# Value matmuls in rounds of four heads, a third bank that VectorE may take, projections issued singly, and 60 transposes by DMA

## The chip, the cores and the metric

The kernel runs on one core of a Trainium2 chip. Five engines work side by side and wait for each other through semaphores: TensorE (PE) for matmuls, ScalarE (ACT) for activations, VectorE (DVE), GpSimd (POOL) and SyncE (SP), which here only issues DMAs. PE writes to PSUM, eight banks of 512 fp32 values in each of 128 partitions. ACT and DVE read it. The metric is device time in microseconds of one execution.

## The reference, cut to what matters

Four layers on a sequence of 2048 tokens of width 512: attention (A), linear attention (B), A, B, each with a layernorm ahead and a residual behind.

```python
x = A_x                                    # [1, 2048, 512], bf16
x = x + _A_ref(_layernorm(x), A_wq, A_wk, A_wv, A_wo)
x = x + _B_ref(_layernorm(x), B_wqkv, B_wo)
x = x + _A_ref(_layernorm(x), A_wq, A_wk, A_wv, A_wo)
x = x + _B_ref(_layernorm(x), B_wqkv, B_wo)

# A: 32 query heads of 16, one shared key and value head
scores = einsum("bhqd,bkd->bhqk", q, k) * 16 ** -0.5
o = einsum("bhqk,bkd->bhqd", softmax(scores), v);   A = o @ wo
# B: phi(t) = where(t > 0, t + 1, exp(t)) + 1e-6
kv = einsum("bhsd,bhse->bhde", phi(k), v);  z = sum_s phi(k)
o = (phi(q) @ kv) / (phi(q) @ z + 1e-6);            B = o @ wo
```

An A layer needs 32 × 2048 × 2048 exponentials. They are most of the kernel's work.

## The kernel before, in words

An A layer is cut into *blocks*: 128 keys against 512 queries of one head, so one 128x512 tile of scores, one PSUM bank. A *segment* (`Seg`) is four heads (`j` = 0 to 3, one for each 32-row strip of TensorE) of one group `g` and one parity, for one stretch of 512 queries `qb`: 16 key tiles x 4 heads = 64 blocks. For `qb` = 0 the keys come in four passes, so that work starts before all keys are known, and those segments have 16 blocks. Each A layer has 2048 blocks, the two together 4096.

Each block goes through a score matmul (line 556, here QK), an exponential and a value matmul (line 568, here PV).

- Banks 0 to 5 form two *sets* of three. `act_stream` (line 581) takes a set, picks three blocks of three heads, issues their QK matmuls as one op, and one exponential on ACT over the three banks (line 627) into one of five `PT` buffers.
- With the QK op a fourth block may go to bank 7. DVE computes its exponential: one pass out of PSUM (line 683, `sV`) for each block, and three passes over pairs of blocks (lines 702, 704, 706) into a `DPT` buffer. `dve_open` (line 666) allows it only if bank 7 is free and nobody waits for it. These blocks come from the next two segments.
- Bank 6 (`ACC`) holds the sums of the value matmuls of the segment at hand, one 32-partition strip for each head. `pv` (line 559) makes one PE op of the blocks of one `PT` buffer (three heads) or of one `DPT` buffer (one or two), and hands it to the planner at once, before their exponentials are done. When all blocks of a segment are handed in, `norms` (line 716) queues the copy or addition out of bank 6 on DVE (lines 727, 729), and `norm` (line 735) *takes a general bank at that moment*, for four transposes (line 742), a reciprocal and a product (lines 750, 754).
- Bank 7 is the only general bank while sets are claimed. Everything else uses it in turn: layernorm transposes (`ln_tile`, line 465), projections (`mm`, line 455, four matmuls in one op), `norm`, the transposes of the attention output (`epilogue`, line 760), and the B layers (`run_b`, line 802).

The order on each engine is fixed when the program is built. A small simulator (`Planner`) runs the kernel with assumed durations (a QK op 0.52 us, a PV op 0.5 us) and, whenever an engine is free, gives it the ready op of the lowest priority number: 0 for QK, 0.5 for `norm`, 2 for PV and `sV`, 3 to 5 for most projections, 8 for DVE's long passes. A few copies (`copy_flex`, line 452) go to ACT or DVE, whichever is free first. On the chip each engine keeps that order, and waits where its inputs are late. B layers are fed as their tiles of x become ready, so most of a B layer runs beside the A layer before it. Only the last 512 rows do not.

Of the kernel before, what the change touches and what calls it, by code (L numbers as in the profile page):

```python
# [17 lines left out]
P = 128  # L18
# [9 lines left out]
class Op:  # L28
    __slots__ = ("eng", "opts", "fn", "deps", "prio", "left", "users", "done", "end", "n", "value", "sem", "signal", "isdma", "name")
# [8 lines left out]
class Planner:  # L38
# [3 lines left out]
    def __init__(self, nc):  # L42
        self.nc = nc
        self.now = 0.0
        self.events = []
        self.seq = 0
        self.ready = {e: [] for e in ENGS}
        self.busy = {e: False for e in ENGS}
        self.order = {e: [] for e in ENGS}
# [10 lines left out]
    def op(self, opts, reads=(), writes=(), prio=5.0, lat=0.08, dma=False, name=""):  # L60

        o = Op()
        o.opts, o.prio, o.users, o.done, o.end = opts, prio, [], False, None
        o.eng, o.fn, o.n, o.value, o.sem, o.signal, o.isdma = None, None, None, None, None, False, dma
        o.name = (name, lat)
        deps = set()
# [18 lines left out]
        o.left = 0  # L85
        for d in deps:
            if not d.done:
# [4 lines left out]
        return o  # L92

# [7 lines left out]
    def _dispatch(self, e):  # L101
        if self.busy[e]:
            return
        h = self.ready[e]
        while h:
            _, _, o = heapq.heappop(h)
            if o.eng is not None:
                continue
            dur, fn = o.opts[e]
            o.eng, o.fn = e, fn  # L110
            self.order[e].append(o)
            self.busy[e] = True
            self.at(self.now + dur, lambda: self._freed(e))
            self.at(self.now + dur + o.name[1], lambda: self._done(o))
            return

    def _freed(self, e):
        self.busy[e] = False
        self._dispatch(e)
# [89 lines left out]
    def finalize(self):  # L209
# [9 lines left out]
        for e in ENGS:  # L219
            c = 0  # L220
            for o in self.order[e]:
                if o.isdma:
                    o.sem = self.nc.alloc_semaphore("s_dma%d" % self.ndma)
                    self.ndma += 1
                    o.value = 16
                elif o.signal:
                    c += 1
                    o.sem, o.value = self.sems[e], c

    def emit(self, e, eng):  # L230
        waited = {}
        for o in self.order[e]:
            need = {}
            for d in o.deps:
                if not d.isdma and d.eng == e and e not in (DV, AC, PO):
                    continue
                k = ("dma", id(d)) if d.isdma else d.eng
# [12 lines left out]
class Seg:  # L250
    def __init__(self, i, qb, g, par, kts, first, last):
# [4 lines left out]
        self.submitted = 0  # L256
        self.emitted = [0] * 4
# [13 lines left out]
QK_DUR = 0.52  # L271
PV_DUR = 0.5
DMAX = 0.5
GA = 3
# [11 lines left out]
def bass_interleave_layers__grouped_kv_mqa__linear_attn_block__prompt_kernel(  # L286
# [32 lines left out]
    NXN = 4  # L319
# [31 lines left out]
    OB = sb("OB", [P, 2, D], BF16)  # L351
    OTB = sb("OTB", [P, 2, 4, P], BF16)
# [14 lines left out]
    banks = Pool_([7, 0, 1, 2, 3, 4, 5])  # L367
    sets = Pool_([])
    retire = {}
    got = {0: [], 3: []}  # L370
    plain_give = pl.give

    def give(pool, item):
        if pool is banks and retire.get(item):
            base = 0 if item < 3 else 3
            got[base].append(item)
            if len(got[base]) == 3:
                got[base] = []
                plain_give(sets, base)
# [5 lines left out]
    def claim_sets():  # L385
        for b in range(6):
            retire[b] = True
        held = [b for b in banks.free if b < 6]
        banks.free = [b for b in banks.free if b >= 6]
# [65 lines left out]
    def mm(dst, pairs, reads, b, prio, dur, stop=True):  # L455
        def fn(e):
            ins = None
            for k, (l, r) in enumerate(pairs):
                ins = e.matmul(dst, lhsT=l, rhs=r, start=(k == 0), stop=(k == len(pairs) - 1))  # L459
            return ins  # L460
        return op({PE: (dur, fn)}, reads=reads, writes=[B_(b)], prio=prio, lat=0.2)
# [3 lines left out]
    def ln_tile(t, prio):  # L465
# [9 lines left out]
           reads=[("x", t), ("mv", t), ("rs", t)], writes=[("xn", i)], prio=prio)  # L475
        b = yield ("acq", banks, prio)
# [13 lines left out]
    def a_tile(L, t, prio):  # L490
        yield ("flag", ("x", L - 1, t))
        yield from ln_tile(t, prio)
# [5 lines left out]
        pl.flag(("V", L, t))  # L498

# [41 lines left out]

    def run_a(L):
# [16 lines left out]
        def pv(sg, items, key, pool, it, holders):  # L559

            yield ("flag", ("acc", L, sg.i))
            for kt, _, _ in items:
                yield ("flag", ("V", L, kt))

            def fn(e):
                ins = None
                for kt, j, ap in items:
# [4 lines left out]
            o = op({PE: (PV_DUR, fn)}, reads=[key] + [("V", kt) for kt, _, _ in items], writes=[B_(ACC)], prio=2.0, lat=0.2)  # L572
            holders[0] -= 1
            holders[1].append(o)
            if holders[0] == 0:
                pl.give_after(pool, it, holders[1])
            sg.submitted += len(items)
            if sg.submitted == sg.total:
                pl.flag(("pv", L, sg.i))

        def act_stream():
            yield from need(segs[0])
            claim_sets()
            while True:
                s_ = yield ("acq", sets, 0.0)
                group = []
                while len(group) < GA and state["si"] < len(segs):
# [22 lines left out]
                extra = dve_open({g_[2] for g_ in group})  # L610
# [10 lines left out]
                op({PE: (QK_DUR, qkx)}, reads=reads, writes=wr, prio=0.0, lat=0.2)  # L621
                if extra is not None:
                    dve_take(extra)
# [5 lines left out]
                pl.give_after(sets, s_, [ex])  # L629
                parts = {}  # L630
                for i, (sg, kt, j) in enumerate(group):
                    parts.setdefault(sg.i, []).append((kt, j, PT[:, p_, i * 512:(i + 1) * 512]))
                hold = [len(parts), []]
                for si, items in parts.items():
                    pl.process(pv(segs[si], items, ("PT", p_), pt_pool, p_, hold))
# [3 lines left out]
        def finish():  # L639
            n = 0  # L640
            while n < 2:
                s_ = yield ("acq", sets, 0.0)
                for b in range(s_, s_ + 3):
# [22 lines left out]
        def dve_open(js):  # L666
            if not USE_DVE or not banks.free or banks.wait:
# [11 lines left out]
        def dve_take(extra):  # L679
# [5 lines left out]
                   writes=[B_(b), ("sV", c_, h)], prio=2.0, lat=0.25)  # L685
            pl.give_after(banks, b, [o])
            if h == 1:
                dve_close()

        def dve_close():  # L690
# [18 lines left out]
            parts = {}  # L709
            for h, (sg, kt, j) in enumerate(blk):  # L710
                parts.setdefault(sg.i, []).append((kt, j, DPT[:, d_, h * 512:(h + 1) * 512]))
            hold = [len(parts), []]
            for si, items in parts.items():
                pl.process(pv(segs[si], items, ("DPT", d_), dp_pool, d_, hold))

        def norms():
            for sg in segs:
                pl.flag(("acc", L, sg.i))
                yield ("flag", ("pv", L, sg.i))
# [15 lines left out]
        def norm(sg, src, key, a_):  # L735
# [3 lines left out]
            def tr(e):  # L739
                ins = None  # L740
                for c in range(4):
                    ins = e.transpose(ps[:, b * 512 + c * P:b * 512 + (c + 1) * P], src[:, c * P:(c + 1) * P], identF[:])  # L742
                return ins
            o = op({PE: (0.8, tr)}, reads=[key, "identF"], writes=[B_(b)], prio=pr, lat=0.2)
# [7 lines left out]
            dst = Osb[:, sg.qb % 2, :].rearrange("p (c g j r d) -> p g r j c d", c=4, g=4, j=4, r=2)[:, sg.g, sg.par]  # L752
# [7 lines left out]
        def epilogue(qb):  # L760
            crit = qb == NB - 1
            pr = 1.0 if crit else 4.0
            for g in range(4):
                for par in range(2):
                    yield ("flag", ("O", L, qb, g, par))
                b = yield ("acq", banks, pr)
                v = bank_bf(b)

                def tr(e, g=g, v=v):
                    ins = None  # L770
                    for c in range(4):
                        ins = e.transpose(v[:, c, :], Osb[:, qb % 2, c * D + g * P:c * D + (g + 1) * P], ident[:])  # L772
# [29 lines left out]
    def run_b(L):  # L802
# [13 lines left out]
        def tile_(t):  # L816
            pr = base(t // 4) + 0.01 * t
            yield ("flag", ("x", L - 1, t))
            yield from ln_tile(t, pr)
# [59 lines left out]
        def main(t):  # L879
# [5 lines left out]
            for h in range(2):  # L885
# [17 lines left out]
                pl.give_after(banks, b, [o])  # L903
            b = yield ("acq", banks, pr)
            v = bank_bf(b)

            def tr(e):
                ins = None
                for g in range(4):
# [5 lines left out]
            b = yield ("acq", banks, pr)  # L915
            m = mm(bank(b), [(OTB[:, i, g, :], wo2[:, g, :]) for g in range(4)], [("OTB", i), "wo2"], b, pr, 0.9)
            pl.give_after(ob_pool, i, [m])
            o = op({DV: (0.62, lambda e: e.tensor_tensor(out=x_sb[:, t, :], in0=x_sb[:, t, :], in1=bank(b), op=ALU.add))},
                   writes=[B_(b), ("x", t)], prio=pr)
            pl.give_after(banks, b, [o])  # L920
            pl.flag(("x", L, t))
# [9 lines left out]
    ob_pool = Pool_(range(2))  # L931
# [48 lines left out]
```

## Time and profile before

| | us |
|---|---|
| three runs: median (lowest to highest) | 2001.18 (1987.07 to 2008.94) |
| the profiled execution: its time | 1994.11 |
| the profiled execution: its span | 1992.4 |
| mean clock granted to TensorE, share of full | 0.734 |

A row of a group gives engine, operation, what is written from what, shapes, count, then the busy time in us, the mean of one in ns, and the idle time just before with what ended it. Busy time counts overlapping instructions once: ACT starts the next instruction before the last has ended, so busy time divided by the count is the pace, and the mean is the latency. A row of stretches gives its bounds and length, then busy us and number of instructions of each engine, the granted clock, and the DMA's share and rate. A row of the timeline gives start, length, engine, line, operation and count of merged instructions, with the idle time before it in brackets.

### The profile page before, as it was taken

Reading aid. Unit: us, or ns where it says so; the run is one execution under the profiler, and the core shown is the slowest. Engines: PE = TensorE matmul, PEld = TensorE weight load, DVE = VectorE, ACT = ScalarE, POOL = GpSimd, SP = SyncE. Lnnn points to the kernel's source line nnn. Section 1 sums busy time; section 2 is a strip of 40 time slices with the busy share of each in tenths; the row PEclk is TensorE's granted clock in tenths of the full one; section 3 lists DMA queues with packets and bytes.
Section 4 is the critical chain, followed back from the end, with each engine's and each line's share of the span. In section 5 each row is a group of like instructions: output and inputs, shape, how many; then the busy total and the mean of one; then the engine's idle time right before and its main releaser. Section 6 shows DMA issues by size and latency. Waiting matters only on the chain.

```text
span 1992.4 us, 25401 instructions
## 1 busy us (share of the span) xinstructions
PE 1631.2 (82%) x10138; PEld 449.5 (23%) x10208; DVE 1209.9 (61%) x1824; ACT 1783.4 (90%) x1392; POOL 40.2 (2%) x89
## 2 busy tenths in 40 slices
PE   7887887888788887887788888878887888878887
PEld 2211222112211122112322222221122111221123
DVE  5389235777387755776544452357763778457757
ACT  7899999999999989996489999999999999899952
POOL 2000000000000000000000000000000000000000
PEclk8857687657966687767778876976679556976668
DMA  3000000000000000000000000000000000000001
GB/s 107 1 1 1 1 1 1 1 1 1 1 1 1 1 1 1 1 1 0 1 1 1 1 1 0 1 1 1 1 1 1 1 1 1 1 1 1 1 1 43
DMA packets 7749, 9.00 MB, mean 5 GB/s; under 512 B 1488, under 2 KB 7120, under 8 KB 7632
## 3 DMA queue, kind: packets, MB, share of 16 engines
q1 hardware_dynamic: 7632, 7.37, 1.1%
q8 instruction: 81, 1.33, 0.3%
q14 instruction: 36, 0.29, 0.0%
HBM read 5.28 MB, written 2.10 MB: 4 GB/s over the span
## 4 chain that ended last, share of the span: by engine, by line
ACT 40%; PE 33%; issue 17%; DVE 9%; DMA 0%; POOL 0%; ACTq 0%; SPq 0%; POOLq 0%
ACT PT L627 37%; PE ps L568 10%; PE ps L556 10%; PE ps L459 7%; PE ps L742 3%; ACT phE L808 2%; DVE sQ L702 1%; DVE sQ L704 1%; DVE sV L683 1%; DVE accS L727 1%; PE ps L772 1%; DVE st L466 1%; DVE phR L809 1%; DVE DPT L706 1%; PE ps L893 1%
## 5 line engine op out<-in xcount | busy, mean ns | idle before, releaser
L627 ACT ACTIVATE PT<-ps 128x1536 bf16<-128x1536 f32 x1264 | 1726.1, 1527 | 87.8 <-PE ps L568 72.3
L556 PE MATMUL ps<-QT,KM 32*128 32x512 bf16 x4096 | 660.8, 501 | 257.8 <-ACT PT L627 236.9
L568 PE MATMUL ps<-PT,V 128*32 128x512 bf16 x3790 | 665.3, 494 | 5.3 <-DVE ve L468 3.1
L556 PEld LDWEIGHTS ps<-QT,KM 32*128 32x128 bf16 x4096 | 134.3, 96 | 806.7 <-ACT PT L627 611.3
L683 DVE TENSOR_SCALAR sV<-ps 128x512 f32<-128x512 f32 x306 | 210.5, 688 | 164.6 <-PE ps L556 164.3
L568 PEld LDWEIGHTS ps<-PT,V 128*32 128x32 bf16 x3790 | 130.9, 98 | 382.8 <-issue 361.7
L704 DVE SCALAR_TENSOR_TENSOR sQ<-sQ,sV 128x1024 f32<-128x1024 f32 (+1 forms) x164 | 189.1, 1153 | 5.5
L702 DVE SCALAR_TENSOR_TENSOR sQ<-sV 128x1024 f32<-128x1024 uint16 (+1 forms) x164 | 189.0, 1153 | 4.9
L706 DVE SCALAR_TENSOR_TENSOR DPT<-sQ,sV 128x1024 int16<-128x1024 f32 (+1 forms) x164 | 187.8, 1145 | 1.0
L809 DVE TENSOR_SCALAR phR<-ps 128x512 f32<-128x512 f32 x64 | 44.0, 691 | 146.8 <-ACT phE L808 146.8
L568 PE MATMUL ps<-DPT,V 128*32 128x512 bf16 x306 | 85.8, 559 | 2.5 <-DVE sacc L729 2.2
L459 PE MATMUL ps<-wqkv,xnT 128*128 128x512 bf16 x233 | 62.9, 395 | 18.4 <-DVE phR L809 12.8
L470 POOL TENSOR_TENSOR rs<-ve,mhalf 128x1 f32<-128x1 f32 x64 | 35.2, 551 | 1891.4 <-DVE ve L468 1882.6
L729 DVE TENSOR_TENSOR sacc<-sacc,ps 128x512 f32<-128x512 f32 x48 | 32.8, 684 | 56.9 <-PE ps L568 56.8
L727 DVE COPY accS<-ps 128x512 f32<-128x512 f32 x48 | 33.1, 690 | 50.3 <-PE ps L568 50.2
L750 DVE RECIPROCAL rden<-ps 128x16 f32<-128x16 f32 x64 | 16.5, 258 | 70.2 <-PE ps L742 69.2
L808 ACT ACTIVATE phE<-ps 128x512 f32<-128x512 f32 x64 | 44.0, 688 | 14.2 <-PE ps L459 13.8
L742 PE MATMUL ps<-identF,accS 128*128 128x128 f32 x192 | 48.0, 398 | 7.9 <-DVE accS L727 7.5
L453 ACT COPY OTB<-ps 128x512 bf16<-128x512 bf16 x20 | 11.7, 585 | 40.9 <-PE ps L910 40.9
L459 PE MATMUL ps<-wo,OTB 128*128 128x512 bf16 x110 | 38.6, 479 | 9.9 <-ACT OTB L453 6.8
L466 DVE BATCH_NORM_STATS2 st<-x_sb 128x6 f32<-128x512 bf16 x64 | 43.6, 684 | 2.9 <-DMA x_sb<-in_A_x_dram 1.9
L482 PE MATMUL ps<-ident,xn 128*128 128x128 bf16 x256 | 27.8, 241 | 20.5 <-DVE xn L473 11.9
(79 smaller groups left out, 759.9 us busy)
## 6 DMA issues: line engine op xcount, KB each, us to landing
out_dram<-x_sb SPq DMA_DIRECT2D x16, 128.0 KB, 1.7
x_sb<-in_A_x_dram SPq DMA_DIRECT2D x3, 512.0 KB, 6.1
wqkv<-in_B_wqkv_dram SPq DMA_DIRECT2D x1, 1536.0 KB, 11.3
x_sb<-in_A_x_dram SPq DMA_DIRECT2D x4, 128.0 KB, 2.3
wq<-in_A_wq_dram SPq DMA_DIRECT2D x1, 512.0 KB, 3.9
wo<-in_A_wo_dram SPq DMA_DIRECT2D x1, 512.0 KB, 8.0
wo<-in_B_wo_dram SPq DMA_DIRECT2D x1, 512.0 KB, 11.3
wk<-in_A_wk_dram SPq DMA_DIRECT2D x1, 16.0 KB, 2.2
```

The costliest lines, as they stand in the source:

```text
L459: ins = e.matmul(dst, lhsT=l, rhs=r, start=(k == 0), stop=(k == len(pairs) - 1))
L466: op({DV: (0.66, lambda e: e.bn_stats(st[:, t, :], x_sb[:, t, :]))}, reads=[("x", t)], writes=[("st", t)], prio=prio)
L556: return e.matmul(bank(b), lhsT=KM[r, sg.par, kt * P:(kt + 1) * P], rhs=QT[r, sg.g, sg.qb * 512:(sg.qb + 1) * 512], start=True, stop=True)
L568: ins = e.matmul(ps[32 * j:32 * j + 32, ACC * 512:(ACC + 1) * 512], lhsT=V[:, kt, :], rhs=ap, start=(sg.emitted[j] == 0), stop=(sg.emitted ...
L627: ex = op({AC: (0.05 + 0.4267 * n, lambda e, n=n, s_=s_, p_=p_: e.activation(PT[:, p_, 0:n * 512], ps[:, s_ * 512:(s_ + n) * 512], ACTF.Ex ...
L683: o = op({DV: (0.60, lambda e: e.tensor_scalar(out=sV[:, c_, h * 512:(h + 1) * 512], in0=bank(b), scalar1=VB, scalar2=VLO, op0=ALU.add, op ...
L702: op({DV: (t_, lambda e: e.scalar_tensor_tensor(out=qq, in0=fr, scalar=CA, in1=fr, op0=ALU.add, op1=ALU.mult))}, reads=keys, writes=[("sQ" ...
L704: op({DV: (t_, lambda e: e.scalar_tensor_tensor(out=qq, in0=qq, scalar=CB, in1=fr, op0=ALU.add, op1=ALU.mult))}, reads=keys, writes=[("sQ" ...
L706: o = op({DV: (t_, lambda e: e.scalar_tensor_tensor(out=DPT[:, d_, 0:n].bitcast(I16), in0=qq, scalar=CK, in1=vv, op0=ALU.mult, op1=ALU.add))},
L742: ins = e.transpose(ps[:, b * 512 + c * P:b * 512 + (c + 1) * P], src[:, c * P:(c + 1) * P], identF[:])
L808: op({AC: (0.55, lambda e: e.activation(phE[:, i, :], bank(b), ACTF.Exp))}, writes=[B_(b), ("phE", i)], prio=min(pr, 0.9))
L809: o = op({DV: (0.62, lambda e: e.tensor_scalar(out=phR[:, i, :], in0=bank(b), scalar1=0.0, scalar2=1e-6, op0=ALU.max, op1=ALU.add))}, writ ...
```

## The change

Six edits. The diff is cut to its core.

1. **PV in rounds of four.** Blocks whose exponential is done are put on the segment's ready list. One PV op takes up to four blocks of four different heads from it, whichever buffer they lie in. It waits for a fourth head unless the rest of the segment is there or `PT` buffers have run out. The next op is formed when the last one starts. `norms` and `norm` are as before, but a segment is now complete only when its last block has been through its exponential.
2. **The third bank.** When two blocks of a group are picked, bank 7 is not to be had, and DVE's backlog is at most 0.2 us by the plan, the third bank goes to DVE (`dve_split`): ACT's exponential then covers two banks, and the set comes free when both ACT and DVE have read it. A block in bank 7 needs a backlog of at most 3 us. Both need all keys of the layer.
3. **Singly.** Projections and `norm`'s transposes are one PE op for each matmul. A PE op no longer waits in the plan for the latency of an earlier PE op. The assumed durations are 0.42 us for QK and 0.36 us for PV.
4. **Transposes by DMA**, issued by SP with an assumed 2.5 us: layernorm tiles 4 to 15 of the first A layer, tiles 0 to 11 of both B layers, and the attention output for `qb` 0 to 2 in both A layers (four each): 12 + 24 + 24 = 60. Each was four PE transposes into a bank and a copy.
5. **Buffers:** `xn` 4 to 6, `OB` and `OTB` 2 to 4. `Osb` is laid out so that one group's 512 columns lie together.
6. **Semaphores:** DMAs share 24 in a ring, and DMA i waits for DMA i - 24.

```diff
-QK_DUR = 0.52
-PV_DUR = 0.5
+QK_DUR = 0.42
+PV_DUR = 0.36
+DTL = 2.5
+FARA = (4, 16)
+FARB = 12
+FARO = 3
+BLS = 0.2
+BLO = 3.0
...
     def mm(dst, pairs, reads, b, prio, dur, stop=True):
...
+        for k, (l, r) in enumerate(pairs):
...
+            o = op({PE: (dur / len(pairs), fn)}, reads=reads, writes=[B_(b)], prio=prio, lat=0.2)
+        return o
...
+    def dmat(dst, src, reads, writes, prio):
+        return op({SP: (0.1, lambda e: e.dma_start(dst, src, transpose=True))}, reads=reads, writes=writes, prio=prio, lat=DTL, dma=True)
...
+        if far:
+            o = dmat(xnT[:, :, t * P:(t + 1) * P], xn[:, i, :], [("xn", i)], [("xnT", t)], prio)
+            pl.give_after(xn_pool, i, [o])
+            return
...
+        def pv_post(src, blk, key, pool, it):
+            hold = [len(blk), [], pool, it]
+
+            def arrived():
+                for sg, kt, j, ap in blk:
+                    sg.ready.append((kt, j, ap, key, hold))
+                pv_kick()
...
+            items, js = [], set()
+            for x in sg.ready:
+                if x[1] not in js and ("V", L, x[0]) in pl.flags:
+                    items.append(x)
+                    js.add(x[1])
...
+            rest = sg.total - sg.submitted
+            if len(items) < 4 and len(sg.ready) < rest and pt_pool.free and not pt_pool.wait and not state["done"]:
+                return
...
+                    if len(group) == GA - 1:
+                        split = dve_split({g_[2] for g_ in group})
+                        if split is not None:
+                            continue
...
-                pl.give_after(sets, s_, [ex])
+                pl.give_after(sets, s_, [ex] if split is None else [ex, p1])
...
-            if not USE_DVE or not banks.free or banks.wait:
+            if not USE_DVE or ("K", L, 3) not in pl.flags or not banks.free or banks.wait or pl.backlog(DV) > BLO:
                 return None
...
+        def dve_split(js):
+            if not USE_DVE or ("K", L, 3) not in pl.flags or (banks.free and not banks.wait) or pl.backlog(DV) > BLS:
+                return None
...
+                if qb < FARO:
+                    dmat(OT[:, g, :].rearrange("p (c q) -> p c q", c=4), Osb[:, qb % 2, g * D:(g + 1) * D],
+                         [("Osb", qb % 2, g, 0), ("Osb", qb % 2, g, 1)], [("OT", g)], pr)
+                    continue
...
-    ob_pool = Pool_(range(2))
+    ob_pool = Pool_(range(NOB))
```

More of the change, by code (lines that the diff above doesn't have):

```diff
@@ L28 @@
 class Op:
-    __slots__ = ("eng", "opts", "fn", "deps", "prio", "left", "users", "done", "end", "n", "value", "sem", "signal", "isdma", "name")
+    __slots__ = ("eng", "opts", "fn", "deps", "prio", "left", "users", "done", "end", "n", "value", "sem", "signal", "isdma", "name", "freed", "begun", "slot")
 class Pool_:
@@ L85, in op @@
         o.left = 0
+        chain = len(opts) == 1 and PE in opts
         for d in deps:
-            if not d.done:
+            if not (d.done or (chain and d.freed and d.eng == PE)):
                 o.left += 1
@@ L92, in op, with backlog @@
         return o
+    def backlog(self, e):
+        left = sum(o.opts[e][0] for _, _, o in self.ready[e] if o.eng is None and len(o.opts) == 1)
+        return left + max(0.0, self.until[e] - self.now)
     def _eligible(self, o):
@@ L112, in _dispatch, with _freed @@
             self.busy[e] = True
-            self.at(self.now + dur, lambda: self._freed(e))
+            self.until[e] = self.now + dur
+            if o.begun:
+                self.at(self.now, o.begun)
+            self.at(self.now + dur, lambda: self._freed(e, o))
             self.at(self.now + dur + o.name[1], lambda: self._done(o))
             return
-    def _freed(self, e):
+    def _freed(self, e, o):
         self.busy[e] = False
+        o.freed = True
+        if e == PE:
+            for u in [u for u in o.users if isinstance(u, Op) and len(u.opts) == 1 and PE in u.opts]:
+                o.users.remove(u)
+                u.left -= 1
+                if u.left == 0:
+                    self._eligible(u)
         self._dispatch(e)
@@ L221, in finalize @@
             for o in self.order[e]:
[L222 to L226, printed above, removed]
+                if not o.isdma and o.signal:
                     c += 1
                     o.sem, o.value = self.sems[e], c
+        dmas = [o for o in self.order[SP] if o.isdma]
+        ring = [self.nc.alloc_semaphore("s_dma%d" % i) for i in range(min(RING, len(dmas)))]
+        for i, o in enumerate(dmas):
+            o.sem, o.value, o.slot = ring[i % RING], 16 * (i // RING + 1), i % RING
+            if i >= RING:
+                o.deps.add(dmas[i - RING])
     def emit(self, e, eng):
@@ L364, in bass_interleave_layers__grouped_kv_mqa__linear_attn_block__prompt_kernel @@
     ACC = 6
-    banks = Pool_([7, 0, 1, 2, 3, 4, 5])
+    NSB = sum(SETS.values())
+    banks = Pool_([7] + [b for b in range(6) if b >= NSB] + list(range(NSB)))
     sets = Pool_([])
     retire = {}
-    got = {0: [], 3: []}
+    got = {b: [] for b in SETS}
     plain_give = pl.give
@@ L385, in claim_sets @@
     def claim_sets():
-        for b in range(6):
+        for b in range(NSB):
             retire[b] = True
-        held = [b for b in banks.free if b < 6]
-        banks.free = [b for b in banks.free if b >= 6]
+        held = [b for b in banks.free if b < NSB]
+        banks.free = [b for b in banks.free if b >= NSB]
         for b in held:
@@ L586, in act_stream @@
                 group = []
-                while len(group) < GA and state["si"] < len(segs):
+                split = None
+                while len(group) < SETS[s_] and split is None and state["si"] < len(segs):
                     sg = segs[state["si"]]
@@ L609, in act_stream @@
                 bk = [B_(s_ + i) for i in range(n)]
-                extra = dve_open({g_[2] for g_ in group})
+                extra = split + (s_ + n,) if split is not None else dve_open({g_[2] for g_ in group})
                 wr = bk
@@ L640, in finish @@
             n = 0
-            while n < 2:
+            while n < len(SETS):
                 s_ = yield ("acq", sets, 0.0)
-                for b in range(s_, s_ + 3):
+                for b in range(s_, s_ + SETS[s_]):
                     retire[b] = False
@@ L684, in dve_take @@
                                                        op0=ALU.add, op1=ALU.max))},
[L685 to L686 removed]
+                   writes=[B_(b), ("sV", c_, h)], prio=2.0 if own else 0.5, lat=0.25)
+            if own:
+                pl.give_after(banks, b, [o])
             if h == 1:
                 dve_close()
+            return o
         def dve_close():
@@ L737, in norm @@
             b = yield ("acq", banks, pr)
[L739 to L744, printed above, removed]
+            for c in range(4):
+                o = op({PE: (0.2, lambda e, c=c: e.transpose(ps[:, b * 512 + c * P:b * 512 + (c + 1) * P], src[:, c * P:(c + 1) * P], identF[:]))},
+                       reads=[key, "identF"], writes=[B_(b)], prio=pr, lat=0.2)
             if a_ is not None:
@@ L903, in main, with otb @@
                 pl.give_after(banks, b, [o])
+            if t >= FARM:
+                o = dmat(OTB[:, i, :, :], OB[:, i, :], [("OB", i, 0), ("OB", i, 1)], [("OTB", i)], pr)
+            else:
+                yield from otb(i, pr)
+            b = yield ("acq", banks, pr)
+            m = mm(bank(b), [(OTB[:, i, g, :], wo2[:, g, :]) for g in range(4)], [("OTB", i), "wo2"], b, pr, 0.9)
+            pl.give_after(ob_pool, i, [m])
+            o = op({DV: (0.62, lambda e: e.tensor_tensor(out=x_sb[:, t, :], in0=x_sb[:, t, :], in1=bank(b), op=ALU.add))},
+                   writes=[B_(b), ("x", t)], prio=pr)
+            pl.give_after(banks, b, [o])
+            pl.flag(("x", L, t))
+        def otb(i, pr):
             b = yield ("acq", banks, pr)
@@ L914, in main @@
             pl.give_after(banks, b, [c])
[L915 to L921, printed above, removed]
         for t in range(T):
```

115 lines of the change are left out of this document (74 added, 41 removed).

## The prediction

> **What bounds the kernel now.** I read the busy table first, then the groups of instructions by shape, then the busy time in stretches, and last the timeline of a few microseconds.
>
> ```profile
> PE 1631.2 (82%) x10138; PEld 449.5 (23%) x10208; DVE 1209.9 (61%) x1824; ACT 1783.4 (90%) x1392; POOL 40.2 (2%) x89
> L627 ACT ACTIVATE PT<-ps 128x1536 bf16<-128x1536 f32 x1262 | 1724.3, 1528 | 87.8 <-PE ps L568 72.3 <-PE ps L556 12.7
> L627 ACT ACTIVATE PT<-ps 128x1024 bf16<-128x1024 f32 x2 | 2.3, 1153 | 0.0
> L683 DVE TENSOR_SCALAR sV<-ps 128x512 f32<-128x512 f32 x306 | 210.5, 688 | 164.6 <-PE ps L556 164.3
> 65.00:905.00 840.00, 694.70 (x4300) 176.65 (x4321) 547.08 (x702) 799.80 (x607) 6.58 (x12) 0.71 0.00 1
> 905.00:985.00 80.00, 57.99 (x315) 22.59 (x319) 45.97 (x104) 35.21 (x44) 4.35 (x8) 0.71 0.00 1
> 985.00:1140.00 155.00, 129.12 (x872) 39.27 (x879) 69.36 (x168) 140.57 (x106) 6.57 (x12) 0.80 0.00 1
> 1140.00:1905.00 765.00, 631.18 (x3932) 163.90 (x3954) 460.18 (x609) 728.37 (x555) 6.58 (x12) 0.73 0.00 1
> 1905.00:1992.40 87.40, 68.70 (x384) 29.73 (x389) 54.05 (x134) 29.54 (x40) 2.16 (x4) 0.81 0.07 25
> ```
>
> The last five rows are the first A layer's body, the turn to the second A layer, that layer's first passes, its body, and the end. In the two bodies ACT is busy for 799.80 of 840 and 728.37 of 765 us: 95%. It is the bound there, and the exponentials are nearly all of it: 1724.3 / 1262 = 1.366 us for three blocks, 0.455 us a block. DVE took 306 of the 4096 blocks and is 65% and 60% busy in the bodies. So the time falls if blocks go from ACT to DVE, and if ACT's 40 + 37 us of idle in the bodies (14 more in the first passes) shrink.
>
> Why does DVE not take more? Two kinds of stretch answer, all engines first, then the `sV` passes alone (one for each block that DVE takes).
>
> ```profile
> 100.00:150.00 50.00, 43.88 (x248) 7.95 (x244) 44.61 (x54) 48.96 (x37) 0.00 (x0) 0.57 0.00 1
> 200.00:250.00 50.00, 41.83 (x245) 12.06 (x245) 11.47 (x25) 46.82 (x35) 0.00 (x0) 0.64 0.00 1
> 400.00:450.00 50.00, 43.47 (x254) 9.96 (x254) 37.78 (x43) 46.91 (x35) 0.00 (x0) 0.57 0.00 1
> 500.00:550.00 50.00, 38.67 (x282) 12.55 (x286) 16.63 (x29) 49.20 (x41) 0.00 (x0) 0.93 0.00 1
> ...
> 100.00:150.00 50.00, 11.66 (x17) 0.57 0.00 1
> 200.00:250.00 50.00, 0.00 (x0) 0.64 0.00 1
> 400.00:450.00 50.00, 10.33 (x15) 0.57 0.00 1
> 500.00:550.00 50.00, 0.69 (x1) 0.93 0.00 1
> ```
>
> From 100 to 150 us DVE takes 17 blocks and is 89% busy. From 200 to 250, the last pass of the first 512 queries, it takes none and is 23% busy, and from 500 to 550, beside the B layer, one. In both, bank 7 is in other hands: the projections and transposes of the B layer use it in turn, and `norm` takes it as soon as a segment's value matmuls are handed to the planner, up to five `PT` buffers before they run. With 16-block segments that is nearly always.
>
> **The change, part by part.**
>
> *More blocks on DVE (edits 1 and 2).* A segment is now complete only when its last exponential is done, so `norm` holds bank 7 for the transposes and little more. And where bank 7 is taken, a group's third bank may go to DVE. I expect DVE as full in both bodies as from 100 to 150 us: 88%. Its passes there, one row of stretches from each of the four lines:
>
> ```profile
> 65.00:905.00 840.00, 114.84 (x167) 0.71 0.00 1
> 65.00:905.00 840.00, 102.78 (x87) 0.71 0.00 1
> 65.00:905.00 840.00, 102.82 (x87) 0.71 0.00 1
> 65.00:905.00 840.00, 101.74 (x87) 0.71 0.00 1
> ...
> 1140.00:1905.00 765.00, 92.23 (x134) 0.73 0.00 1
> L453 DVE COPY xnT<-ps 128x512 bf16<-128x512 bf16 x52 | 21.9, 422 | 30.6 <-PE ps L482 30.6
> L453 DVE COPY OT<-ps 128x512 bf16<-128x512 bf16 x30 | 12.7, 424 | 26.2 <-PE ps L772 26.2
> ```
>
> The first four sum to 422.2 us for 167 blocks: 2.53 us a block. DVE's other work in this body is 547 - 422 = 125 us. With the second body's 134 blocks (the last `sV` row) at the same price, the other work there is 460 - 339 = 121 us. Of these 246 us some 45 copies of 0.42 us go to the DMA: 227 us are left. The bodies are 1605 us long and, by the sum below, some 85 shorter afterwards: 1520 x 0.88 = 1338 us, less 227, by 2.53 gives 439 blocks, 133 more than the 306. The first passes of the second layer stay without, since DVE must wait for that layer's last keys.
>
> What a block saves depends on its bank. One in bank 7 leaves a full group: 0.455 us. A split only shortens the exponential, 1528 to 1153 ns: 0.375 us. If 110 are splits and 23 more go through bank 7, ACT saves 41 + 10 = **51 us**. The price on DVE is hidden by its idle time. If that cover is gone, a set waits for DVE: one long pass (1.2 us) and its own `sV` (0.69 us) against an exponential of 1.15 us. That is up to 0.75 us late, while ACT has the other set (1.37 us) to work on, so I take nothing here. At worst it costs 110 x 0.4 = 44 us.
>
> *PV in rounds of four (edit 1).* Before, each of 1264 groups and 164 pairs was at least one round: 1428. Four blocks a round make at least 1024, some 1100 with the ends of segments. What a round costs, first at a halved clock, then at the full one:
>
> ```profile
> 643.91 0.61 PE L556 MATMUL ps<-QT,KM 32*128 32x512 bf16 x4 [0.28 <-ACT PT L627]
> 644.45 0.61 PE L568 MATMUL ps<-PT,V 128*32 128x512 bf16 x3
> 645.16 0.61 PE L556 MATMUL ps<-QT,KM 32*128 32x512 bf16 x3
> 513.32 0.39 PE L556 MATMUL ps<-QT,KM 32*128 32x512 bf16 x3
> 513.63 0.40 PE L568 MATMUL ps<-PT,V 128*32 128x512 bf16 x3
> 513.97 0.40 PE L482 MATMUL ps<-ident,xn 128*128 128x128 bf16 x4
> ACT PT L627 <- PE ps L568: 72.3, 78, 5.2
> ```
>
> A round takes the place of the next one after 0.54 us at the halved clock (643.91 to 644.45), 0.32 at the full one. A group needs a QK round and before 1.13 PV rounds or more: 1.15 us of ACT's 1.366 at the halved clock, before norms and projections. Afterwards 1100 PV rounds for some 1250 groups make it 1.02. The last row is where ACT pays today: 72 of its waits end with a PV matmul, since an exponential needs a `PT` buffer that PV must free. With a quarter of the rounds gone, and a QK round never behind more than one matmul of a projection, I take 40 of the 91 us of idle (bodies and first passes) as gone: **40 us**. The ends are none and all.
>
> The profile row of the clock: 0.57 where PE is 43.47 of 50 us busy, 0.93 where it is 38.67, so busy time is long because the clock is low. The Trainium skill, "TensorE: Matmul & The Clock Gate", The HAM clock gate, says that the clock is halved by default and that activity releases it; by that, fewer rounds mean a lower clock. The trace agrees as far as full-array projections go with the high rows, and that becomes the second rival below.
>
> *Singly.* The same matmuls. If each stands between other rounds, a projection takes four fills in place of one; PE has the room, so nothing. Without the room see the second rival.
>
> *Transposes by DMA.* 60 x 4 transposes and 60 copies go. On PE four take 0.40 us (the row at 513.97), hidden; the copies are counted above. ACT loses at most 14 of them and gets others from a fuller DVE: nothing. What is new is a wait: a projection stands in PE's fixed order behind a DMA that the plan expects after 2.5 us. No transpose by DMA is in the trace. The rows of other DMAs:
>
> ```profile
> out_dram<-x_sb SPq DMA_DIRECT2D x16, 128.0 KB, 1.7
> x_sb<-in_A_x_dram SPq DMA_DIRECT2D x3, 512.0 KB, 6.1
> wqkv<-in_B_wqkv_dram SPq DMA_DIRECT2D x1, 1536.0 KB, 11.3
> x_sb<-in_A_x_dram SPq DMA_DIRECT2D x4, 128.0 KB, 2.3
> ```
>
> The same 128 KB take 1.7 to 2.3 us; 11.3 is the far end. The plan itself runs slower on the chip (a group planned at 1.33 us takes 1.366 at best), and ACT forgives some 0.35 us (1.366 - 1.02). I take 3.0 us, near the rows of that size, which costs 0.2 us at each of 42 waits (36 layernorm tiles, and the last of four outputs in six epilogues): **8 us**. Behind a late one wait QK and then ACT. SP's queue holds nothing else between the loads and the stores.
>
> The Trainium skill, "Advanced Engine Details and Errata", X-Bar Transpose (TRN2), says that such DMAs are as fast as regular ones; no run here shows it yet, and by it the 8 us would be none.
>
> *Buffers, semaphores.* In the turn and at the end (80 + 87 us) main tiles of B go in pairs of `OB` buffers; four should take some **8 us** off both together (0.25 us for each of 32 tiles, an estimate). The ring is never full with 60 + 27 DMAs in 1.9 ms: nothing.
>
> Sum: 1992.4 - 51 - 40 + 8 - 8 = 1901 us of span. The profiled execution stands at 1994.11, 1.7 above its span and 7 under the median of its runs. That gives **1903 us** beside it, and up to 1910 beside the median. I say 1905.
>
> **The rivals.**
>
> *The DMAs are late (slower).* If a transpose lands after 6.1 us, as the 512 KB loads do, each of 42 waits costs 6.1 - 2.5 - 0.35 = 3.25 us, 136 in all: 1893 + 136 = 2029 us. It decides from a landing of some 5 us on (42 x 2.15 = 90 us, all that is gained). At 11.3 us it would be 2248. For it: a transpose moves every 2-byte element to another partition, which no transfer of before does, and PE keeps a fixed order. Against it: 128 KB rows of 1.7 and 2.3 us.
>
> *PE becomes the bound (no change).* If fewer, more scattered rounds leave the clock at half, 200 projections of four matmuls (36 in an A layer, 64 in a B layer, by the code) take 1.9 in place of 1.04 us:
>
> ```profile
> 509.29 0.39 PE L556 MATMUL ps<-QT,KM 32*128 32x512 bf16 x3 [0.42 <-ACT PT L627]
> 1955.44 1.89 PE L459 MATMUL ps<-wo,OTB 128*128 128x512 bf16 x4
> 1970.86 1.04 PE L459 MATMUL ps<-wo,OTB 128*128 128x512 bf16 x4
> ```
>
> That is 0.85 us each, less the 0.35 that ACT forgives: 200 x 0.5 = 100 us, the whole gain and a little more: 2001 us of span. Against it: the clock rises to 0.93 wherever projections run today.
>
> *Everything goes (much faster).* DVE at 95% gives (1444 - 227) / 2.53 = 481 blocks and 67 us, and all 91 us of idle vanish: 1992 - 158 - 8 = 1826.
>
> *DVE does not fill.* With no more blocks and the rest as above: 1954. It lies inside the range.
>
> **How the numbers follow.** The forecast with its own range of 1850 to 1960: 0.66. Late DMAs above 2020: 0.11. PE the bound, within 1%: 0.09. Much faster, under 1850: 0.14. The range, 1825 to 1985, takes in the far end of the gains and stops short of both losing rivals. One per cent, 20 us, is about what three runs of this kernel (1987 to 2009) can tell. Faster 0.80, same 0.09, slower 0.11.
>
> **What would show it.** Right: some 440 `sV` passes, about 110 exponentials over two banks, DVE near 88% in both bodies, PV rounds mostly of four, ACT's waits on PV under 40 us, DMAs landing near 3 us. Wrong: waits of PE on a transposed tile or `OT` in the table of waits; waits of QK on `sV`; a clock near 0.55 throughout; or DVE still idle from 200 to 250 us.

## The result, and the profile after

The changed kernel takes 1932.18 us (median of four runs, 1930.72 to 1932.82) against 1996.22 us before. The ratio is 0.967, 95% interval 0.962 to 0.973. Run again beside later experiments, it came to 0.968 (0.965 to 0.971). The forecast was faster, 1905 us within 1825 to 1985, so some 90 us less than before. Of the span, 61 us came off (1992.4 to 1931.1).

The busy table and the groups of the changed kernel, then its two bodies, its end and the stretch from 200 to 250 us (all engines, columns as before; the bounds of the stretches are set by eye):

```profile
PE 1540.5 (80%) x9968; PEld 406.9 (21%) x9968; DVE 1524.5 (79%) x2161; ACT 1729.9 (90%) x1402; POOL 43.3 (2%) x89
...
L718 ACT ACTIVATE PT<-ps 128x1536 bf16<-128x1536 f32 x1078 | 1490.7, 1467 | 64.2 <-PE ps L599 44.4 <-PE ps L646 16.7
...
L782 DVE TENSOR_SCALAR sV<-ps 128x512 f32<-128x512 f32 x461 | 316.3, 687 | 156.7 <-PE ps L599 155.1
...
L718 ACT ACTIVATE PT<-ps 128x1024 bf16<-128x1024 f32 x200 | 207.4, 1063 | 22.3 <-PE ps L646 14.2 <-PE ps L599 7.6
```

```profile
62.00:850.00 788.00, 624.09 (x4097) 153.91 (x4096) 674.67 (x842) 753.38 (x599) 8.69 (x12) 0.69 0.02 5
...
1105.00:1845.00 740.00, 593.96 (x3868) 145.92 (x3865) 625.57 (x790) 701.58 (x561) 8.11 (x13) 0.69 0.02 5
1845.00:1931.10 86.10, 68.36 (x390) 29.59 (x390) 52.11 (x132) 30.26 (x40) 2.20 (x4) 0.79 0.07 25
...
200.00:250.00 50.00, 44.14 (x252) 11.58 (x253) 41.33 (x59) 45.46 (x36) 0.21 (x1) 0.53 0.06 11
```

DVE takes 461 blocks, 200 of them as third banks, and is 86% and 85% busy in the bodies. From 200 to 250 us, where it had done nothing for the exponentials, it is 83% busy. All exponentials together now keep ACT busy for 1674.5 us in place of 1726.1. So ACT lost 52 us of work, and with its other work 53.5 (1783.4 to 1729.9). What did not shrink is its idle time: 1992.4 - 1783.4 = 209.0 us before, 1931.1 - 1729.9 = 201.2 after. In the bodies it stood at 40.2 + 36.6 us and stands at 34.6 + 38.4.

The tables of waits say why. First the kernel before, then the changed one (who waits, for whom: us in total, times, longest):

```profile
ACT PT L627 <- PE ps L556: 12.7, 30, 1.5
...
PE ps L556 <- ACT PT L627: 236.9, 577, 1.1
```

```profile
ACT PT L718 <- PE ps L599: 52.0, 123, 1.2
...
ACT PT L718 <- PE ps L646: 30.8, 26, 2.4
...
PE ps L646 <- ACT PT L718: 209.5, 425, 1.4
PE ps L599 <- ACT PT L718: 74.2, 201, 1.2
...
PE ps L599 <- DVE sV L782: 2.2, 6, 0.5
```

ACT's waits on value matmuls fell from 72.3 to 30.8 us, by about the 40 that were forecast. Its waits on score matmuls rose from 12.7 to 52.0, by 39. One took the place of the other. The rows of PE show what changed there: before, score matmuls waited for ACT, and value matmuls followed them. Now it is mostly the value matmuls (L646) that wait for ACT. A score matmul hardly ever waits for VectorE's `sV` (2.2 us). The timeline of the changed kernel, at the halved clock:

```profile
564.20 0.62 PE L646 MATMUL ps<-PT,V 128*32 128x512 bf16 x4 [0.64 <-ACT PT L718]
...
564.74 0.61 PE L599 MATMUL ps<-QT,KM 32*128 32x512 bf16 x3
...
565.54 0.62 PE L646 MATMUL ps<-PT,V 128*32 128x512 bf16 x4 [0.18 <-ACT PT L718]
...
566.09 0.61 PE L599 MATMUL ps<-QT,KM 32*128 32x512 bf16 x4
```

An exponential ends and releases two things: a set for the next scores, and a buffer for the value round. The value round now stands first in PE's order, and the scores start 0.54 us later (564.20 to 564.74). In the plan the round is formed in the same instant, by a shorter path of events than the next group, and PE is free, so it goes out first in spite of its lower priority.

The transposing DMAs of the changed kernel, with a load of the same size between them, and the only waits of PE on them (its weight loads, PEld):

```profile
xnT<-xn SPq DMA_TRANSPOSE x36, 2.4
x_sb<-in_A_x_dram SPq DMA_DIRECT2D x4, 128.0 KB, 2.4
...
OT<-Osb SPq DMA_TRANSPOSE x24, 2.4
```

```profile
PEld ps L491 <- DMA xnT<-xn: 0.5, 2, 0.2
...
PEld ps L491 <- DMA OT<-Osb: 0.4, 1, 0.4
```

Their median is 2.4 us, under the planned 2.5 (the longest took 7.3 us), and they cost 0.9 us of waits in all.

### The profile page after: what moved, and what is told of

Read it like the earlier page. It is cut to its first block, busy times and chain, and to the rows that moved or that the text cites. A ratio compares the mean times of both kernels' runs of the same rounds, so it can differ in the third digit from the quotient of the medians.

```text
span 1931.1 us, 25551 instructions
## 1 busy us (share of the span) xinstructions
PE 1540.5 (80%) x9968; PEld 406.9 (21%) x9968; DVE 1524.5 (79%) x2161; ACT 1729.9 (90%) x1402; POOL 43.3 (2%) x89
## 4 chain that ended last, share of the span: by engine, by line
ACT 35%; PE 34%; issue 17%; DVE 13%; DMA 0%; POOL 0%; ACTq 0%; SPq 0%; POOLq 0%; DVEq 0%
ACT PT L718 33%; PE ps L646 11%; PE ps L599 11%; PE ps L491 7%; PE ps L837 3%; DVE sQ L805 2%; DVE sV L782 2%; DVE sQ L803 2%; DVE DPT L807 1%; DVE phR L907 1%; ACT phE L906 1%; DVE accS L824 1%; DVE sacc L826 1%; PE ps L991 1%; PE ps L989 1%
## 5 line engine op out<-in xcount | busy, mean ns | idle before, releaser
L718 ACT ACTIVATE PT<-ps 128x1536 bf16<-128x1536 f32 (+1 forms) x1279 | 1674.5, 1403 | 86.5 <-PE ps L599 52.0
L646 PE MATMUL ps<-PT,V 128*32 128x512 bf16 x3635 | 560.1, 519 | 214.1 <-ACT PT L718 204.8
L782 DVE TENSOR_SCALAR sV<-ps 128x512 f32<-128x512 f32 x461 | 316.3, 687 | 156.7 <-PE ps L599 155.1
L803 DVE SCALAR_TENSOR_TENSOR sQ<-sV 128x1024 f32<-128x1024 uint16 (+1 forms) x243 | 282.9, 1164 | 4.5
L805 DVE SCALAR_TENSOR_TENSOR sQ<-sQ,sV 128x1024 f32<-128x1024 f32 (+1 forms) x243 | 282.2, 1162 | 3.0
L807 DVE SCALAR_TENSOR_TENSOR DPT<-sQ,sV 128x1024 int16<-128x1024 f32 (+1 forms) x243 | 282.1, 1161 | 2.8
L646 PEld LDWEIGHTS ps<-PT,V 128*32 128x32 bf16 x3635 | 111.8, 99 | 558.1 <-ACT PT L718 417.0
L646 PE MATMUL ps<-DPT,V 128*32 128x512 bf16 x461 | 123.6, 563 | 8.4 <-ACT PT L718 4.7
L505 POOL TENSOR_TENSOR rs<-ve,mhalf 128x1 f32<-128x1 f32 x64 | 38.4, 603 | 1829.6 <-DVE ve L503 1821.2
L1009 DVE TENSOR_TENSOR x_sb<-x_sb,ps 128x512 bf16<-128x512 bf16 x32 | 22.0, 688 | 41.1 <-PE ps L491 40.5
L491 PE MATMUL ps<-wo,OT 128*128 128x512 bf16 x128 | 42.3, 434 | 3.3 <-DVE x_sb L881 1.7
L491 PE MATMUL ps<-xnT,wqkv 128*128 128x512 bf16 x128 | 38.6, 411 | 5.2 <-DVE phR L907 3.5
```

What stands on the lines that cost most here:

```text
L491: return e.matmul(dst, lhsT=l, rhs=r, start=(k == 0), stop=(k == len(pairs) - 1))
L646: ins = e.matmul(ps[32 * j:32 * j + 32, ACC * 512:(ACC + 1) * 512], lhsT=V[:, kt, :], rhs=ap, start=(sg.emitted[j] == 0), stop=(sg.emitted ...
L718: ex = op({AC: (0.05 + 0.4267 * n, lambda e, n=n, s_=s_, p_=p_: e.activation(PT[:, p_, 0:n * 512], ps[:, s_ * 512:(s_ + n) * 512], ACTF.Ex ...
L782: o = op({DV: (0.60, lambda e: e.tensor_scalar(out=sV[:, c_, h * 512:(h + 1) * 512], in0=bank(b), scalar1=VB, scalar2=VLO, op0=ALU.add, op ...
L803: op({DV: (t_, lambda e: e.scalar_tensor_tensor(out=qq, in0=fr, scalar=CA, in1=fr, op0=ALU.add, op1=ALU.mult))}, reads=keys, writes=[("sQ" ...
L805: op({DV: (t_, lambda e: e.scalar_tensor_tensor(out=qq, in0=qq, scalar=CB, in1=fr, op0=ALU.add, op1=ALU.mult))}, reads=keys, writes=[("sQ" ...
```

## The experiments

Each group of four ran on one chip, with the kernel before beside it. The first group is scores first, no third bank, transposes back, and VectorE from the first passes on; the second is the changed kernel again, scores first without a third bank, projections as one op, and rounds by buffer; the rest is the third. The kernel before had a median of 2012, 1996 and 1992 us beside them, so ratios are what to compare across groups.

**Scores first.** A value round is formed a moment later in the plan, so that the group which the same exponential releases goes ahead:

```diff
                 for sg, kt, j, ap in blk:
                     sg.ready.append((kt, j, ap, key, hold))
-                pv_kick()
+                pl.at(pl.now + 0.02, pv_kick)
```

> The changed kernel, but a value round is formed 0.02 us (of the plan) after its blocks arrive, so that the score matmuls which the same exponential releases go into TensorE's order ahead of it. Theory 1 (order): in the changed kernel the value round stands first and waits for the exponential, so the score matmuls start one round (0.32 to 0.54 us) late, which is why ACT's waits on score matmuls rose from 12.7 to 52.0 us. Then these waits fall below 25 us and the time falls by 25 to 40 us, to 1892 to 1907. Theory 2 (sets held by VectorE's third banks) and theory 3 (the lower clock, 0.70 in place of 0.73): the waits stay near 50 us and the time within 10 us of 1932.

It took 1892.1 us, ratio 0.942 (0.937 to 0.947): 2.6% below the changed kernel, as theory 1 has it. Its busy table, waits and timeline:

```profile
PE 1517.9 (80%) x9968; PEld 401.1 (21%) x9968; DVE 1529.4 (81%) x2176; ACT 1713.1 (91%) x1403; POOL 45.0 (2%) x89
...
L718 ACT ACTIVATE PT<-ps 128x1536 bf16<-128x1536 f32 x1068 | 1475.1, 1514 | 44.2 <-PE ps L599 25.8 <-PE ps L646 15.4
```

```profile
ACT PT L718 <- PE ps L599: 36.7, 74, 1.2
...
ACT PT L718 <- PE ps L646: 18.2, 17, 1.6
...
PE ps L599 <- ACT PT L718: 248.9, 538, 1.1
```

```profile
545.70 0.61 PE L599 MATMUL ps<-QT,KM 32*128 32x512 bf16 x3
...
546.24 0.62 PE L646 MATMUL ps<-PT,V 128*32 128x512 bf16 x4
...
548.38 0.61 PE L599 MATMUL ps<-QT,KM 32*128 32x512 bf16 x3 [0.64 <-ACT PT L718]
...
548.92 0.62 PE L646 MATMUL ps<-PT,V 128*32 128x512 bf16 x4
```

Scores wait for ACT again, and value rounds follow. ACT is idle for 1890.2 - 1713.1 = 177.1 us, 24 less. All exponentials keep it busy for 1660.0 us, 14.5 less, with only four blocks fewer: one that starts late does not overlap the one before it, and that loss counts as busy time. In the trace of the kernel before, an exponential over three banks that starts after a wait takes 1.45 us; one that starts while the last still runs takes 1.54, but the next start is 1.33 us behind its own. So the mean latency tells how often they overlap: 1528 ns before, 1467 in the changed kernel, 1514 here. The waits on scores fell to 36.7 us and not below 25, so part of that expectation failed. The 40 us between the medians are 51 by the ratios.

**No third bank.** `dve_split` always returns `None`:

```diff
         def dve_split(js):
...
+            return None
```

> The changed kernel without the third bank for VectorE: blocks go to VectorE through bank 7 only. The program then has 332 VectorE blocks in place of 461, and nearly all exponentials cover three banks. By the prediction's prices ACT gets 129 blocks more at 0.455 us less what shorter exponentials lose, about 50 us, so 1975 to 1985. Theory 2 (a set waits for VectorE): ACT's waits on score matmuls fall from 52 to 20 us or less, and the time rises by only 15 to 25 us, 1947 to 1957. Theory 1 (order): the waits stay above 40 us and the time is 1975 to 1985.

1954.3 us, ratio 0.975 (0.969 to 0.980), waits on scores 30.8 us. The time lies in theory 2's range, the waits between the two.

```profile
ACT PT L718 <- PE ps L599: 30.8, 80, 1.0
ACT PT L718 <- PE ps L646: 27.9, 26, 2.3
```

Without the splits ACT is busy 44 us longer (1773.9), but idle 22 us less (1953.0 - 1773.9 = 179). So the splits give half of their gain back, or two thirds by the ratios, which differ by only 0.7% and have intervals that just overlap.

**Scores first and no third bank.** Both edits above.

> Score matmuls first, as in e1_qk_first, and no third bank for VectorE. Without the splits alone, ACT's waits on score matmuls fell from 52 to 31 us, so something about splits makes score matmuls late. Theory 2 (a set is held until VectorE has read its third bank): in e1 the 36.7 us that are left are that, and fall below 18 us here. Theory 1b (a two-bank exponential covers only 1.0 us, less than a value round and a score round after each other at the halved clock, 1.15 us; once the scores go first this is mended): they stay within 8 us of 36.7. The splits are worth 14 to 22 us without the new order; with it, by theory 1b, 30 to 45 us, so this kernel takes 1922 to 1937; by theory 2 1905 to 1917.

1940.8 us, ratio 0.971 (0.968 to 0.974).

```profile
ACT PT L718 <- PE ps L599: 31.6, 68, 1.2
ACT PT L718 <- PE ps L646: 29.7, 22, 2.5
```

Theory 2 falls: the waits that the first experiment left (36.7) stay within the bound of theory 1b without a single split. The time is above both ranges. So the third bank is worth 0.7% in the changed kernel's order (0.975 against 0.968) and 2.9% with scores first (0.971 against 0.942). Read the other way, scores first is worth 2.6% with splits and next to nothing without them (0.975 and 0.971, with intervals that overlap; waits on scores 30.8 and 31.6 us). As far as these runs can tell, the order costs time only together with the splits.

That agrees with theory 1b: a two-bank exponential takes 207.4 / 200 = 1.04 us, and a value round and a score round one after the other take 0.54 + 0.61 at the halved clock. Where exponentials overlap in the changed kernel, the next start is 1.35 us behind a full one, which covers these 1.15 us, and 0.93 us behind one over two banks, which does not (medians of the trace). ACT's timeline tells the two theories apart as well. A wait for want of cover comes right behind a two-bank exponential; a wait for a held set comes one exponential later, when that set is due again. Sorted so, about 22 us of the changed kernel's waits on scores come right behind a two-bank exponential, 1 us comes one later, and 32 us have none in the last two, as many as without splits (33).

In that kernel, with neither splits nor value rounds ahead of the scores, 31.6 us remain where the kernel before had 12.7. This rest has another cause, which no run here settles.

**Transposes back on TensorE.**

```diff
-FARA = (4, 16)
-FARB = 12
-FARO = 3
+FARA = (16, 16)
+FARB = 0
+FARO = 0
```

> The changed kernel with all 60 transposes on TensorE again, as before the change. The prediction put them at 8 us of loss; they land in 2.4 us, so a wait for them should cost nothing, and without them 60 copies and 60 uses of bank 7 come back. The program has 449 VectorE blocks in place of 461: 12 x 0.375 = 5 us more on ACT, and some waits for bank 7. Expected 1932 to 1950. If the DMAs cost anything, it is below 1927.

1941.5 us, ratio 0.967 (0.962 to 0.972), the changed kernel's own ratio. The 60 DMAs cost nothing and bring nothing that can be told.

**Projections as one op again** (`mm` as before the change; `norm`'s transposes stay single).

> The changed kernel with projections of four matmuls as one op again. The prediction held the single issue at nothing in itself, with the waits of ACT behind projections in its 40 us. There are 200 projections, and a score round may stand up to 1.04 us (full clock) behind one. Expected: 5 to 20 us slower than the changed kernel on this chip; if single issue costs fills that matter, 5 us or more faster.

1940.2 us, ratio 0.972 (0.969 to 0.974), beside 1932.9 and 0.968 (0.965 to 0.971) for the changed kernel on the same chip. Seven us slower, with intervals that overlap: at the low end of what was expected, and not settled.

**Value rounds by buffer**, with no waiting for a fourth head:

```diff
-                if x[1] not in js and ("V", L, x[0]) in pl.flags:
+                if x[1] not in js and ("V", L, x[0]) in pl.flags and (not items or x[3] == items[0][3]):
...
-            if len(items) < 4 and len(sg.ready) < rest and pt_pool.free and not pt_pool.wait and not state["done"]:
-                return
```

> The changed kernel with a value round for the blocks of one buffer at a time, as before the change, formed as soon as they have arrived. The program of before has 1516 such rounds, the changed one 1159. If the rounds of four relieve TensorE, as the prediction has it, their loss brings ACT's waits on value matmuls back from 31 us to 60 or more and 20 to 45 us of time. If TensorE has room for them, as its 80% busy would say, the time stays within 10 us.

1918.7 us, ratio 0.960 (0.958 to 0.963): *faster* than the rounds of four, by 14 us on the same chip. Neither expectation held. Waits on value matmuls stayed (31.7 us), waits on scores fell to 35.2, and the clock rose. The mean granted clock of the profiled executions:

| | span, us | clock | share of the time at half |
|---|---|---|---|
| before | 1992.4 | 0.734 | 0.53 |
| changed, run again beside this one | 1930.4 | 0.702 | 0.60 |
| rounds by buffer | 1918.0 | 0.771 | 0.46 |
| scores first | 1890.2 | 0.718 | 0.56 |
| scores first, rounds by buffer | 1886.7 | 0.781 | 0.44 |

The traces record the clock in stretches, 134 in the changed kernel, and every one is at 1 or at 0.5. So the share of the time at half is twice what is missing to 1. Whether that is a loss of its own was tried by putting the order right first, and by feeding the clock with work that changes nothing.

**Scores first and rounds by buffer.**

> Score matmuls first (e1_qk_first, 1892) and value rounds by buffer (e4_pv_by_buffer, 1919) together. If the order and the clock are two separate losses of the changed kernel, the gains add: 40 + 14 us below 1932, so 1875 to 1885, with the share of time at half clock below 0.50 (0.61 in the changed kernel, 0.57 in e1, 0.46 in e4). If e4 gained only because its smaller rounds come sooner, the order has that gain already: 1888 to 1900.

1888.1 us, ratio 0.948 (0.944 to 0.951), with the clock at 0.781. That is what scores first alone has (0.942, 0.937 to 0.947). The gains do not add. What the waits gain on one side they lose on the other:

```profile
ACT PT L716 <- PE ps L599: 19.2, 43, 1.0
ACT PT L716 <- PE ps L644: 34.4, 31, 2.3
```

With rounds of four, scores first had 36.7 us on scores and 18.2 on value matmuls.

**Score matmuls issued twice**, in the changed kernel, with scores first, and with scores first and rounds by buffer:

```diff
-                    for i, (sg, kt, j) in enumerate(group):
-                        ins = qk_mm(e, s_ + i, sg, kt, j)
+                    for _ in range(2):
+                        for i, (sg, kt, j) in enumerate(group):
+                            ins = qk_mm(e, s_ + i, sg, kt, j)
```

> The changed kernel with the score matmuls of each group issued twice into the same banks, which changes no value. TensorE gets a third more 512-wide matmuls. Theory 3 (rounds of four lower the clock, and the slow rounds make scores late): the clock rises from 0.70 to 0.9 or more, ACT's waits on score matmuls fall below 35 us, and the time falls to 1905 to 1925 in spite of the added work. If the clock plays no part, the added round of 0.21 to 0.43 us stands before every exponential, and the time rises to 1960 or more.

> Score matmuls first, and each issued twice. Theory 3: clock above 0.9, rounds follow each other at 0.32 us in place of 0.54, and the time falls below 1892 to 1865 to 1885. Without an effect of the clock: 1910 or more.

> Score matmuls first and twice, and value rounds by buffer. By theory 3 the clock is near full already with the scores twice, and then more value rounds cost TensorE time and bring nothing: within 10 us of e13. If smaller rounds help for another reason (they free buffers sooner), 10 us or more below e13.

| | us | ratio (interval) | clock | ACT's waits on scores, us |
|---|---|---|---|---|
| changed kernel, scores twice | 2020.1 | 1.014 (1.010 to 1.019) | 0.800 | 106.3 |
| scores first, twice | 1923.4 | 0.964 (0.959 to 0.969) | 0.858 | 52.2 |
| scores first, twice, rounds by buffer | 1878.6 | 0.941 (0.937 to 0.946) | 0.953 | 15.9 |

Theory 3 fails in the first two: the clock rises by 0.10 and 0.14, and so does the time, from a ratio of 0.967 to 1.014 and from 0.942 to 0.964. Here the added matmuls ahead of an exponential counted for more than the higher clock. In the first the same added round costs about twice as much, which fits that the value round stands ahead of it as well. Only with all three does the clock come near full. That kernel is 45 us faster than the one without rounds by buffer on the same chip, where 10 were the bound, and its interval overlaps that of scores first alone. How much of the 45 us is the clock, and how much that smaller rounds are shorter, these runs do not tell apart.

**VectorE from the first passes on**, without the condition on all keys in `dve_open` and `dve_split`:

> The changed kernel without the condition that VectorE takes blocks only when all keys of the layer are there. In the first passes of the second A layer VectorE is busy for 73 of 170 us and takes no block. The program has 483 VectorE blocks in place of 461. At 0.375 us each 8 us less: 1924, unless VectorE then delays the B layer's tail, whose tiles the passes wait for: 1932 to 1945.

1961.8 us, ratio 0.977 (0.972 to 0.981), worse than both expectations; by the ratios it is 0.9% slower than the changed kernel, with intervals that just overlap. The first passes of the second A layer, in the changed kernel and here (bounds by eye):

```profile
935.00:1105.00 170.00, 143.28 (x938) 42.11 (x939) 73.41 (x181) 145.57 (x114) 7.66 (x14) 0.69 0.00 1
```

```profile
940.00:1130.00 190.00, 151.23 (x934) 41.55 (x932) 121.42 (x223) 146.70 (x129) 8.92 (x12) 0.63 0.00 1
```

DVE is 48 us busier there, ACT works as long, and the stretch is 20 us longer. That would be 20 of the 28 us of span. The B layer's last tiles go through the same bank 7 and the same DVE, and the passes wait for them; that this is the cause was not tried by itself. Waits on scores rose too (67.3 us over the whole run).

## Why the prediction held, and where its sum was off

The time lies in the range, 27 us above the 1905 that the sum gave. ACT's work came down as forecast, and the idle time hardly moved.

*Blocks for VectorE:* right in the total. 439 were worked out from DVE at 88%; it came to 461 at 85 to 86%. ACT's saving was put at 51 us and is 51.6 (1726.1 to 1674.5). That the two agree so closely is partly luck, since the way was another: not 110 splits and a gain of 23 blocks through bank 7, but 200 splits and fewer blocks through bank 7 than before (261 against 306). By the prediction's prices that mix gives 200 x 0.375 - 45 x 0.455 = 54.5 us. Without splits the program has 332 blocks, so `norm` freeing bank 7 sooner is worth little by itself.

*The 40 us of idle* is the step that failed. "With a quarter of the rounds gone, and a QK round never behind more than one matmul of a projection, I take 40 of the 91 us of idle (bodies and first passes) as gone." The waits on value matmuls fell by 41.5, as said. But the step looked at how many rounds there are and not at what stands first in PE's queue when an exponential ends, and 39 us of new waits on scores took the place. The runs divide these 39. About 21 came with the splits, whose price on ACT the prediction put at nothing ("ACT has the other set (1.37 us) to work on"): a split shortens just that cover, and the value round had moved ahead of the scores. Scores first takes away 15 of them, and with shorter waits on value matmuls and more overlap brings the ratio to 0.942, below the forecast (1905 is 0.954 of the 1996 measured before). The other 18 stand without splits and in either order. What brought them stays open. With scores first and rounds by buffer 19.2 us of waits on scores are left, so the rounds of four, or the lower clock seen with them, have a part in it. Without splits ACT's idle time is 30 us under that before (179 against 209), so three quarters of the 40 were there and the splits took 22 back. The text did list "waits of QK on `sV`" as a sign; they are 2.2 us.

One row was misread: "72 of its waits" are 72.3 us in 78 waits. The sum does not use the count.

*Rounds of four:* 1159 in the program against 1516, near the 1100 forecast. PE's busy time fell by 6%. With scores first they do shorten the waits on value matmuls (18.2 us, by buffer 34.4), but the waits on scores are as much longer, and rounds by buffer are as good there, and better in the changed kernel's order.

*PE becomes the bound*, the second rival, did not come, though the clock fell from 0.734 to 0.699. The rule of the Trainium skill, "TensorE: Matmul & The Clock Gate", The HAM clock gate, that activity releases the clock, would have it so for less activity, and the runs with added matmuls agree (0.953 at the most). With scores first, rounds by buffer raised the clock by 0.06 and the number of value rounds with it, and the time stayed. What the clock alone is worth stays open.

*Late DMAs*, the first rival: excluded. Forecast 3.0 us and 8 us of loss; measured 2.4 (the median) and 0.9. The Trainium skill, "Advanced Engine Details and Errata", X-Bar Transpose (TRN2), says that they are as fast as regular ones, and this trace agrees: a 128 KB load takes 2.4 us as well.

*Singly:* put at nothing, and 7 us on the border of what can be told. *Buffers:* put at 8 us in the turn and the end; they were not tried by themselves, and the 8 us are not to be seen. From the end of the first A layer's last exponential to the start of the second's first it is 60.0 us and was 59.4; from the last exponential to the end of the span it is 72.3 us and was 76.0.

So the sum took off 51, 40 and 8 us and put 8 on, 91 in all; 61.3 came off, 53.5 of ACT's work and 7.8 of its idle time.

## What to carry to other kernels

When one event releases work for two successors on the same in-order engine, look which of them stands first: the one that feeds the bound engine should, and priorities in a planner do not see to it if the other becomes ready a moment earlier in its event order. Here that cost time only where the bound engine's own work in hand was too short to cover both, so a change that shortens its instructions can uncover a wait that was hidden. After a change, compare the waits of the bound engine by releaser, not their sum: a wait that goes and a wait that comes can cancel to within 2 us. And fewer, fuller matmul rounds were no gain here, where TensorE was not the bound.

## What the runs showed that was not expected

Issuing the score matmuls twice, with scores first and rounds by buffer, made the kernel no slower (0.941 against 0.948, with intervals that overlap), while the granted clock rose from 0.781 to 0.953. Without rounds by buffer the same added matmuls took the ratio from 0.942 to 0.964, at a clock of 0.858.
